# Block transposes on VectorE and sixteen SBUF transfers for two of six query tiles of a bucketed attention with a mixture of experts behind it

## The chip, the cores and the metric

One core of one Trainium2 chip runs the whole program in one launch. The metric is device microseconds (us) from start to end of an execution. The kernel before takes 754.33 us (median of three runs, 753.67 to 754.85).

## The reference

Attention over 4 batches and 8 heads, 768 tokens, 64 features a head: each query and key gets a bucket of six sign bits, and a query sees only the keys of its bucket. Behind it a mixture of eight experts, one expert for a token.

```python
def _attn_ref(q, k, v, proj):                     # q, k, v: 4 x 8 x 768 x 64, proj: 64 x 6
    q_bits = (np.einsum('bhsd,dk->bhsk', q, proj) > 0)
    k_bits = (np.einsum('bhsd,dk->bhsk', k, proj) > 0)
    q_bucket, k_bucket = (np.sum(b * 2 ** np.arange(6), axis=-1) for b in (q_bits, k_bits))
    mask = q_bucket[:, :, :, None] == k_bucket[:, :, None, :]
    scores = np.where(mask, np.matmul(q, k.transpose(0, 1, 3, 2)) / 8, -1e9)
    attn = np.exp(scores - np.max(scores, axis=-1, keepdims=True))
    attn = attn / (np.sum(attn, axis=-1, keepdims=True) + 1e-09)
    return np.matmul(attn, v)
# x: the 3072 tokens x 512 features of the above
# expert = argmax(x @ w_gate), gate = its softmax; out = gate * (relu(x @ w1[expert]) @ w2[expert])
```

## The kernel before, in words

**Groups and units.** The attention runs over 16 groups g of two heads. A group has 12 units i: a unit is 128 queries of one head against all 768 keys. Units 0 to 5 are the first half of the queries (three query tiles t of two heads s), units 6 to 11 the second half. In groups 1 to 15 units 2c and 2c+1 are the two heads of one query tile, so pair c = 0 to 5 is a query tile.

**The steps of a unit**, each a letter in a hand-written order (`HEAD` for group 0, `PLAN` for groups 1 to 14, `LAST` for group 15). The order is each engine's program order: all engines take their instructions in it, and only semaphores hold them back. A trailing `-` means the step belongs to the group before.

- S (`score`): four TensorE matmuls of 384 columns into a PSUM tile `s` (three of them). The mask comes in as 16 extra rows of the operands (line 285).
- R (`peak`, lines 295 to 297): VectorE takes the row maximum from PSUM and makes bias and scale of it. Each second R also puts work on GpSimd (`behind`): two of the twelve pieces (`split`) that prepare the operands of the next group's scores, and behind the eighth of them the two mask loads (`mask`, line 258).
- X (`expo`, line 305): ScalarE takes the exponential, `s` to the SBUF tile `e` (four of them).
- T (`trans`, line 319): for a pair c and k = 0, 1, 2, four TensorE transposes of 128 x 128 of `e` into a PSUM tile `t` (two of them, shared with all other small products).
- E (`trans_ev`, lines 343 and 345): the eviction of that tile to `pt`, by ScalarE (a) or VectorE (v).
- V (`pv`, line 355): the product of `pt` with the values, one for each half of a group, V0 and V1: 24 matmul instructions into a `t`. O (line 360) evicts it, K (`tok`, line 374) turns it into rows by token with the router's columns, L (line 384) scales and stores it with the reciprocals of M.
- G, H: the product with the six projections for the next group, and its signs on ScalarE. H also calls `lsh_bits` (line 253): GpSimd scales the bits, a transfer writes them to DRAM (`md`, line 254, SyncE's queue), and `mask` reads them back in another layout.

**Loads.** `before`, called at every second S, puts the loads of later groups on SyncE's queue: `load_x` (line 76, two of 768 KB a group), `load_pair` (line 81, 768 KB), `load_v` (line 86, 384 KB), and in groups 1 and 2 four `fill` each (line 149, 1156 KB to DRAM).

**Behind the attention.** After each batch of four groups, `route` counts the tokens of each expert and `scatter` (line 448, GpSimd's queue) writes them to DRAM sorted by expert. The experts' part (lines 641 to 799) starts at about 440 us. There, `xt_blocks` already turns 32 x 32 blocks on VectorE (line 679), from tiles that four transfers of 32 partitions each have filled (line 641).

Of the kernel before, what the change touches and what calls it, by code (L numbers as in the profile page):

```python
# [53 lines left out]
def lsh_attention_moe(ctx, tc, qk, qk2, v, proj, wg, w1, w1p, w2, out):  # L54
# [256 lines left out]
    def trans(c, k):  # L311

        i = 2 * c
        e = PP[i], PP[i + 1]
        p = ps.tile([128, 512], F32, name="t", bufs=2)
        for x in range(4):
            w, j = (x % 2, x // 2) if i in (0, 4) else (x // 2, x % 2)
            kt = 2 * k + j
            nc.tensor.transpose(p[:, x * 128:(x + 1) * 128],  # L319
                                e[w][:, kt // 3, (kt % 3) * 128:(kt % 3) * 128 + 128], ident)  # L320
        TB[c, k] = p
        if k == 2:
            del PP[i], PP[i + 1]

    def trans_ev(c, k, vec):

        p = TB.pop((c, k))
        u = c // 3
        if u not in PT:
            PT[u] = wk.tile([128, 2, NT, HALF], F32, name="pt")  # L330
        pt = PT[u]
        _, _, s, t = unit(2 * c)
        ks, q = slice(2 * k, 2 * k + 2), slice(t * 128, t * 128 + 128)
        if c in (0, 2):
            parts = [(pt[:, s, ks, t * 128:t * 128 + 256], p.rearrange("p (k q) -> p k q", k=2))]
        elif c == 1:
            parts = [(pt[:, w, ks, (2 - 2 * w) * 128:(3 - 2 * w) * 128],
                      p[:, w * 256:(w + 1) * 256].rearrange("p (k q) -> p k q", k=2)) for w in range(2)]
# [514 lines left out]
    def weight_half(op, x):  # L853
# [31 lines left out]
    """.split()  # L885

    PLAN = """
        S0 E40a- L0- X11- T41- R0 T42- E41a- S1 E42a- G X0 R1 T50- H S2 E50a- S3 X1 R2 T51- T52- E51a- S4 E52v- X2
        T00 R3 T01 E00a S5 E01a R4 T02 X3 V1- R5 X4 E02a X5 T10 O1- S6 E10a T11 R6 T12 E11a S7 E12a T20 X6 T21 E20v
        S8 E21a R7 T22 S9 E22a R8 K1- X7 V0 R9 X8 X9 M1- L1- M0 T30 O0 S10 E30a T31 R10 T32 E31a S11 E32a T40 X10  # L890
        R11 K0
    """.split()

    LAST = """
# [5 lines left out]
        r1 m6 r1 u5 u6 tV c0 m7 u7 tV d5 d6 tP c1 d7  # L900
    """.split()

    DEAL = {"R5": 1, "E12a": 2, "T20": 1, "R8": 1, "M0": 1}

    def route_step(g, w):

        b, q = divmod(g - NP, NP)
        if b < 0 or b >= B - 1:
            return
        if q == 0 and w == "M0":  # L910
            routes[b] = route(b, (0, 1))
            go(routes[b], 1)
        if q == 1:
            go(routes[b], DEAL.get(w, 0))
        if q == 2 and w in ("R0", "R2"):
            scatter(b, w == "R2")

    def before(c):

        g, r = divmod(c, 6)  # L920
        if g + 2 < NG and r in (0, 2) and g + 2 != NG - 1:
            load_x(2 * g + 4 + r // 2)
        if g == NG - 2 and r == 0:
            load_x(2 * g + 2)
            load_x(2 * g + 3)
# [4 lines left out]
        if g in (1, 2) and r > 1:  # L930
            fill((g - 1) * 4 + r - 2)

    def behind(i):

# [14 lines left out]
            weights((1, 1, 1, 2, 1, 2)[c - NC + 6])  # L949

    TK = {}

    def step(g, w):

        prev = w.endswith("-")
        w = w.rstrip("-")
        n = g - prev
        if n < 0 or (g == NG and not prev):
            return
        op, x = w[0], w[1:]  # L960
        if op == "S":
            i = 12 * n + int(x)
# [3 lines left out]
        elif op == "R":  # L966
            i = 12 * n + int(x)
            peak(i)
            behind(i)
        elif op == "X":  # L970
            expo(12 * n + int(x))
        elif op == "T":
            trans(6 * n + int(x[0]), int(x[1]))
        elif op == "E":
            trans_ev(6 * n + int(x[0]), int(x[1]), x[2] == "v")
        elif op == "V":
            for kt in range(NT):
                pv(2 * n + int(x[0]), kt)
        elif op == "O":
            pv_end(2 * n + int(x))  # L980
        elif op == "M":
            sums(2 * n + int(x))
        elif op == "K":
            TK[2 * n + int(x)] = tok(2 * n + int(x))
        elif op == "L":
            tok_ev(2 * n + int(x), TK.pop(2 * n + int(x)))
        elif op == "G" and n + 1 < NG:
            lsh_mm(n + 1)
        elif op == "H" and n + 1 < NG:
            lsh_ev(n + 1)  # L990
            if n:
                lsh_bits(n + 1)
        elif op in "kjqlp":
            cut(op, int(x[0]), int(x[1]), x[2])
        elif op == "y":
            lsh_first(int(x[0]), int(x[1]))
        elif op == "b":
            bits_first(int(x[0]), int(x[1]))
        elif op == "f":
            if x == "0":  # L1000
                before(0)
            score(0, (x == "1",))
        elif op == "i":
            if int(x[0]) not in SC:
                SC[int(x[0])] = ps.tile([128, 2, 512], F32, name="s", bufs=3)
            warmth(SC[int(x[0])][:, 0], int(x[1]))
        elif op == "s":
            split(2 + int(x[0]), int(x[1]))
        elif op == "z":
            mask(2 + int(x))  # L1010
        elif op == "w":
            lsh_bits(1)
        elif op in "xgh":
# [12 lines left out]
    last = [route(B - 1, (0,)), route(B - 1, (1,))]
    for g in range(NG):
        for w in HEAD if g == 0 else LAST if g == NG - 1 else PLAN:
            step(g, w)
            route_step(g, w)  # L1030
            if g == NG - 2 and w in ("R5", "R7", "M0", "R11"):
                next(pick, None)
                if w == "R11":
                    raw_load(0, 0)
                    raw_load(0, 1)
            if g == NG - 1 and w == "R9":
# [126 lines left out]
```

## Time and profile before

| | us |
|---|---|
| median of three runs | 754.33 |
| lowest, highest | 753.67, 754.85 |
| the profiled execution | 755.68 |
| span of its instructions | 753.9 |
| attention, groups 1 to 14: from one V0 to the next | 27.1 to 27.4 |

The profiled execution took 1.8 us more than its span from the first to the last instruction. It is 1.35 us above the median. Times of rows count from the start of the span.

### The profile page before, as it was taken

Reading aid. Unit: us, or ns where it says so; the run is one execution under the profiler, and the core shown is the slowest. Engines: PE = TensorE matmul, PEld = TensorE weight load, DVE = VectorE, ACT = ScalarE, POOL = GpSimd, SP = SyncE. Lnnn points to the kernel's source line nnn. Section 1 sums busy time; section 2 is a strip of 40 time slices with the busy share of each in tenths; the row PEclk is TensorE's granted clock in tenths of the full one; section 3 lists DMA queues with packets and bytes.
Section 4 is the critical chain, followed back from the end, with each engine's and each line's share of the span. In section 5 each row is a group of like instructions: output and inputs, shape, how many; then the busy total and the mean of one; then the engine's idle time right before and its main releaser. Section 6 shows DMA issues by size and latency. Waiting matters only on the chain.

```text
span 753.9 us, 13381 instructions
## 1 busy us (share of the span) xinstructions
PE 745.7 (99%) x4723; PEld 616.2 (82%) x4723; DVE 456.5 (61%) x1042; ACT 483.2 (64%) x942; POOL 470.5 (62%) x575
## 2 busy tenths in 40 slices
PE   9999999999999999999999999999999999999997
PEld 5778777777787787877778788889999999989896
DVE  7766766767676676676688775254383925262421
ACT  7879878878887887887887761464344444453410
POOL 6867355578635768735766643576666666668532
PEclk9999999999999999999999999999999999999999
DMA  8499844235325335422343323956636476736401
GB/s 283 168 315 277 280 128 168 83 133 193 128 64 168 121 111 200 154 75 67 101 173 116 116 73 134 253 160 189 155 135 170 144 131 181 188 135 170 147 9 38
DMA packets 60181, 113.71 MB, mean 151 GB/s; under 512 B 12227, under 2 KB 27715, under 8 KB 60112
## 3 DMA queue, kind: packets, MB, share of 16 engines
q1 hardware_dynamic: 53280, 96.47, 42.3%
q0 software_dynamic: 6688, 16.35, 6.4%
q8 instruction: 38, 0.62, 0.4%
q14 instruction: 31, 0.25, 0.1%
q10 hardware_dynamic: 144, 0.02, 0.0%
HBM read 86.98 MB, written 26.33 MB: 150 GB/s over the span
## 4 chain that ended last, share of the span: by engine, by line
PE 90%; issue 3%; DMA 2%; POOL 1%; DVE 1%; ACT 1%; POOLq 0%; DVEq 0%; SPq 0%; ACTq 0%
PE t L319 17%; PE t L355 17%; PE s L729 15%; PE s L766 10%; PE s L287 9%; PE s L285 9%; PE s L786 6%; PE t L374 3%; DMA raw<-in_w1p_dram 2%; PE t L243 2%; PE s L795 1%; POOL w L625 1%; PE t L105 1%; DVE xh L682 1%; ACT e L305 0%
## 5 line engine op out<-in xcount | busy, mean ns | idle before, releaser
L295 DVE TENSOR_REDUCE m<-s 128x1 f32<-128x768 f32 x192 | 182.9, 952 | 94.8 <-PE s L287 85.6
L305 ACT ACTIVATE e<-s,m 128x768 f32<-128x768 f32 x192 | 191.2, 996 | 16.6 <-DVE m L297 9.8
L625 POOL TENSOR_TENSOR w<-raw,w 128x512 fp32r<-128x512 f32 x112 | 144.6, 1317 | 39.7 <-ACT w L624 39.1
L345 ACT ACTIVATE pt<-t 128x512 f32<-128x512 f32 (+1 forms) x253 | 142.9, 593 | 28.9 <-PE t L319 25.1
L319 PE MATMUL t<-ident,e 128*128 128x128 f32 x1152 | 160.6, 275 | 0.6 <-ACT e L305 0.4
L319 PEld LDWEIGHTS t<-ident,e 128*128 128x128 f32 x1152 | 132.6, 140 | 33.9 <-issue 12.6
L355 PE MATMUL t<-pt,vt 128*64 128x384 f32 x768 | 130.9, 490 | 0.0
L729 PE MATMUL s<-xh,w 128*128 128x456 f32 (+6 forms) x672 | 127.0, 346 | 0.7 <-DVE xh L682 0.7
L729 PEld LDWEIGHTS s<-xh,w 128*128 128x128 f32 x672 | 119.1, 188 | 4.1 <-DVE xh L682 1.0
L355 PEld LDWEIGHTS t<-pt,vt 128*64 128x64 f32 x768 | 52.2, 137 | 62.2 <-issue 60.1
L745 DVE SCALAR_TENSOR_TENSOR hh<-s,hh 128x256 fp32r<-128x256 f32 (+7 forms) x64 | 35.5, 555 | 110.8 <-ACT hh L743 109.6
L743 ACT ACTIVATE hh<-s 128x256 fp32r<-128x256 f32 (+7 forms) x64 | 31.3, 490 | 83.1 <-PE s L729 83.1
L766 PE MATMUL s<-hh,w 128*128 128x456 f32 (+3 forms) x384 | 74.9, 355 | 0.0
L624 ACT ACTIVATE w<-raw 128x512 fp32r<-128x512 f32 x112 | 66.4, 623 | 11.7 <-DMA raw<-in_w1p_dram 11.5
L766 PEld LDWEIGHTS s<-hh,w 128*128 128x128 f32 x384 | 71.1, 188 | 2.6
L799 POOL DMA_INDIRECT out_dram<-y,ix x26 | 25.9, 998 | 62.4 <-DVE y L797 37.3
L786 PE MATMUL s<-w,hh 128*128 128x512 f32 (+1 forms) x240 | 56.7, 395 | 0.8 <-ACT hh L743 0.8
L285 PE MATMUL s<-w 80*128 80x384 f32 x192 | 57.0, 378 | 0.0
L285 PE MATMUL s<-qk 80*128 80x384 f32 x192 | 56.3, 375 | 0.0
L786 PEld LDWEIGHTS s<-w,hh 128*128 128x128 f32 (+1 forms) x240 | 44.5, 187 | 11.7 <-ACT hh L743 1.3
L287 PE MATMUL s<-qk 128*128 128x384 f32 x192 | 50.0, 341 | 0.0
L253 POOL TENSOR_SCALAR bits<-bits,wsg 64x384 f32<-64x384 f32 x15 | 18.7, 1245 | 50.2 <-ACT bits L226 50.2
(202 smaller groups left out, 1018.4 us busy)
## 6 DMA issues: line engine op xcount, KB each, us to landing
raw<-in_w_dram SPq DMA_DIRECT2D x36, 512.0 KB, 3.7
raw<-in_w1p_dram SPq DMA_DIRECT2D x28, 512.0 KB, 3.8
xd<-in_qk_dram SPq DMA_DIRECT2D x16, 768.0 KB, 4.3
xhe<-in_qk_dram SPq DMA_DIRECT2D x15, 768.0 KB, 7.6
w<-in_qk_dram SPq DMA_DIRECT2D x14, 768.0 KB, 4.4
sorted_rows<-xr SPq DMA_DIRECT2D x8, 1156.0 KB, 14.5
vt<-in_v_dram SPq DMA_DIRECT2D x16, 384.0 KB, 3.9
masks<-bits SPq DMA_DIRECT2D x15, 192.0 KB, 1.9
```

The source lines that it names most:

```text
L285: nc.tensor.matmul(p[:, a, :HALF], k[0:80, 2, c], k[0:80, 3, n], start=i >= 4, stop=i < 4)
L287: nc.tensor.matmul(p[:, a, :HALF], k[:, 0, c], k[:, 1, n], start=i < 4, stop=i >= 4)
L295: nc.vector.tensor_reduce(m[:, 0:1], p[:, :, :HALF], axis=AX.XY, op=OP.max)
L305: nc.scalar.activation(e, p[:, :, :HALF], AF.Exp, bias=m[:, 2:3], scale=m[:, 1:2], accum_out=SM[g, hf][:, t, s:s + 1])
L319: nc.tensor.transpose(p[:, x * 128:(x + 1) * 128], e[w][:, kt // 3, (kt % 3) * 128:(kt % 3) * 128 + 128], ident)
L345: nc.scalar.activation(o, x, AF.Copy)
L355: nc.tensor.matmul(p[s * 64:(s + 1) * 64, :HALF], VT[g][:, kt, s, :], PT[u][:, s, kt, :], start=(kt == 0), stop=(kt == NT - 1))
L624: nc.scalar.activation(w[:, 0, a], r, AF.Copy)
L625: nc.gpsimd.tensor_tensor(w[:, 1, a], r, w[:, 0, a], op=OP.subtract)
L729: nc.tensor.matmul(p[:, :c], w[:, a, d, fs], x[:, b, d, :c], start=(k == 0), stop=(k == 11))
L766: nc.tensor.matmul(p[:, :c], w[:, a, f % 4, ms], h[b][:, f, :c], start=(k == 0), stop=(k == 23))
L786: nc.tensor.matmul(p[:pw], HH[n][b][:, f, i:i + pw], w[:, a, f % 4], start=(k == 0), stop=(k == 23))
```

## The change

In groups 1 to 14, the pairs c = 0 and 1 (units 0 to 3) are no longer transposed by TensorE. A new step D (`blocks`) turns each of the four units in 32 x 32 blocks on VectorE, from `e` to a tile `z` (in the place of `w2`, or `w0` in group 14). After the fourth, sixteen transfers on SyncE's queue carry blocks from each quarter of 32 partitions to each other quarter of `pt`: 32 partitions of 3072 B, 98 KB each. The layout of `pt` changes so that a transfer is contiguous in it: the 384 queries of a half lie as 4 quarters of 3 tiles of 32. So the matmul of V reads its moving operand in runs of 32, the transposes write `t` in runs of 32, and the evictions write runs of 64. In group 0, whose units 0 to 5 lie in another order, each eviction of its first three pairs is two instructions of 256 columns.

The loads of a group stand together behind the transfers (step I), with two fills each in groups 1 to 4. The write of the bits to `md` goes to GpSimd's queue. `PLAN` is new: the last transposes of a group, R11, X10, X11, V0 and V1 now run in the next group, K1 and L1 in the one after it (`--`); `END` closes group 14; `DONE` keeps a step from running twice. The routing steps of a batch move to one group.

```diff
-        nc.sync.dma_start(md[g], r)
+        (nc.gpsimd if g > 1 else nc.sync).dma_start(md[g], r)
...
+        o = p.rearrange("p (a w j i) -> p j w a i", j=2, w=2, a=4)
         for x in range(4):
...
-            nc.tensor.transpose(p[:, x * 128:(x + 1) * 128],
+            nc.tensor.transpose(o[:, j, w],
                                 e[w][:, kt // 3, (kt % 3) * 128:(kt % 3) * 128 + 128], ident)
...
+    def pt_tile(u):
+        if u not in PT:
+            PT[u] = wk.tile([128, 4, 3, 2, NT, 32], F32, name="pt")
+        return PT[u]
...
+    def blocks(i):
+
+        g, r = divmod(i, 12)
+        c, w = divmod(r, 2)
+        if r == 0:
+            ZT[g] = moe.tile([128, 4, 2, 2, NT * 32], F32, name="w2" if g < NG - 2 else "w0")
+        z = ZT[g]
+        e = PP.pop(i).rearrange("p h c -> p (h c)").rearrange("p (k g j) -> p g k j", g=4, j=32)
+        nc.vector.transpose(z[:, :, c, w].rearrange("p g (k i) -> p g k i", i=32), e)
+        if r == 3:
+            pt = pt_tile(2 * g)
+            for a in range(4):
+                for q in range(4):
+                    nc.sync.dma_start(pt[32 * q:32 * q + 32, a, 0:2].rearrange("p t s k i -> p (t s k i)"),
+                                      z[32 * a:32 * a + 32, q].rearrange("p c w x -> p (c w x)"))
...
+        x = p.rearrange("p (a w x) -> p a w x", w=2, a=4)
+        if c < 3:
+            parts = []
+            for w in range(2):
+                _, _, s, t = unit(2 * c + w)
+                parts.append((pt[:, :, t, s, ks].rearrange("p a k i -> p a (k i)"), x[:, :, w]))
         else:
-            parts = [(pt[:, :, ks, q], p.rearrange("p (s k q) -> p s k q", s=2, k=2))]
+            parts = [(pt[:, :, c % 3, :, ks].rearrange("p a s k i -> p a s (k i)"), x)]
...
-            nc.tensor.matmul(p[s * 64:(s + 1) * 64, :HALF], VT[g][:, kt, s, :], PT[u][:, s, kt, :],
+            nc.tensor.matmul(p[s * 64:(s + 1) * 64, :HALF], VT[g][:, kt, s, :],
+                             PT[u][:, :, :, s, kt].rearrange("p a t i -> p t a i"),
...
     PLAN = """
-        S0 E40a- L0- X11- T41- R0 T42- E41a- S1 E42a- G X0 R1 T50- H S2 E50a- S3 X1 R2 T51- T52- E51a- S4 E52v- X2
-        T00 R3 T01 E00a S5 E01a R4 T02 X3 V1- R5 X4 E02a X5 T10 O1- S6 E10a T11 R6 T12 E11a S7 E12a T20 X6 T21 E20v
-        S8 E21a R7 T22 S9 E22a R8 K1- X7 V0 R9 X8 X9 M1- L1- M0 T30 O0 S10 E30a T31 R10 T32 E31a S11 E32a T40 X10
-        R11 K0
+        S0 R11- E32a- K1-- X10- T40- L1-- X11- S1 E40v- T41- R0 T42- E41a- S2 M1- V0- X0 R1 E42a- R2 X1 D0
+        T50- O0- D1 S3 E50a- T51- R3 T52- E51a- S4 X2 G R4 X3 S5 E52a- S6 R5 X4 V1- H D2 X5 D3 I R6 S7 O1-
+        X6 T20 R7 T21 E20a S8 E21a M0- T22 X7 R8 S9 K0- E22a R9 X8 T30 S10 E30a L0- S11 X9 R10 T31 T32 E31a
     """.split()
...
-    DEAL = {"R5": 1, "E12a": 2, "T20": 1, "R8": 1, "M0": 1}
+    DEAL = {"R4": 1, "R5": 1, "R6": 1, "R7": 1, "R8": 1, "R9": 1}
...
+    def loads(g):
+
+        if g + 2 < NG - 1:
+            load_x(2 * g + 4)
+            load_x(2 * g + 5)
+        if g + 2 < NG:
+            load_pair(g + 2)
+        if g + 1 < NG:
+            load_v(g + 1)
...
+    END = ["K1-", "L1-", "R11", "E32a", "X10", "T40", "V0", "O0", "M0", "K0"]
...
+        elif op == "I":
+            loads(n)
+            if n < 5:
+                fill(2 * n - 2)
+                fill(2 * n - 1)
```

## Rows read from the trace of the kernel before

**Rows 1.** The page: busy time by engine, TensorE's clock in 40 slices.

```profile
PE 745.7 (99%) x4723; PEld 616.2 (82%) x4723; DVE 456.5 (61%) x1042; ACT 483.2 (64%) x942; POOL 470.5 (62%) x575
...
PEclk9999999999999999999999999999999999999999
```

**Rows 2.** The chain that ended last: shares of the span by line.

```profile
PE t L319 17%; PE t L355 17%; PE s L729 15%; PE s L766 10%; PE s L287 9%; PE s L285 9%; PE s L786 6%; PE t L374 3%; DMA raw<-in_w1p_dram 2%; PE t L243 2%; PE s L795 1%; POOL w L625 1%; PE t L105 1%; DVE xh L682 1%; ACT e L305 0%
```

**Rows 3.** V0 to V0: us, PE PEld DVE ACT POOL busy, PEclk, DMA share, GB/s.

```profile
50.17:77.25 27.08, 27.08 (x190) 20.75 (x192) 18.34 (x45) 22.41 (x44) 15.31 (x19) 1.00 0.96 309
...
284.23:311.32 27.09, 27.09 (x191) 20.76 (x192) 18.33 (x45) 22.39 (x44) 19.45 (x24) 1.00 0.45 149
...
365.57:392.94 27.37, 27.37 (x197) 20.89 (x199) 19.50 (x52) 22.54 (x45) 18.65 (x32) 1.00 0.42 140
```

**Rows 4.** TensorE in order of time, within one group: start, us, instructions.

```profile
289.39 1.04 PE L319 MATMUL t<-ident,e 128*128 128x128 f32 x8
290.18 0.60 PE L285 MATMUL s<-qk 80*128 80x384 f32 x2
...
290.97 1.04 PE L319 MATMUL t<-ident,e 128*128 128x128 f32 x8
...
294.51 4.09 PE L355 MATMUL t<-pt,vt 128*64 128x384 f32 x24
298.53 0.66 PE L319 MATMUL t<-ident,e 128*128 128x128 f32 x4
```

**Rows 5.** VectorE in order of time, same group: two R one behind the other.

```profile
293.51 0.95 DVE L295 TENSOR_REDUCE m<-s 128x1 f32<-128x768 f32 x1
...
294.81 0.95 DVE L295 TENSOR_REDUCE m<-s 128x1 f32<-128x768 f32 x1
```

**Rows 6.** ScalarE in order of time, same group.

```profile
305.01 1.00 ACT L305 ACTIVATE e<-s,m 128x768 f32<-128x768 f32 x1
...
305.98 0.59 ACT L226 ACTIVATE bits<-t,small 128x384 f32<-128x384 f32 x1
306.44 0.62 ACT L345 ACTIVATE pt<-t 128x512 f32<-128x512 f32 x1
306.92 1.03 ACT L305 ACTIVATE e<-s,m 128x768 f32<-128x768 f32 x1
```

**Rows 7.** VectorE's block transposes of the experts' part, by shape.

```profile
L679 DVE STREAM_TRANSPOSE xt<-xb 128x384 f32<-128x384 f32 x12 | 6.2, 551 | 0.0
...
L679 DVE STREAM_TRANSPOSE xt<-xb 128x480 f32<-128x480 f32 x4 | 2.5, 650 | 0.0
```

**Rows 8.** Instructions by line and shape, 284.2 to 311.3 us.

```profile
L345 ACT ACTIVATE pt<-t 128x512 f32<-128x512 f32 x16 | 9.1, 596 | 1.9 <-PE t L319 1.7
...
L343 DVE COPY pt<-t 128x512 f32<-128x512 f32 x2 | 1.4, 692 | 0.7 <-PE t L319 0.6
L253 POOL TENSOR_SCALAR bits<-bits,wsg 64x384 f32<-64x384 f32 x1 | 1.2, 1244 | 5.1 <-ACT bits L226 5.1
```

**Rows 9.** GpSimd's scatter issues, 240 to 400 us.

```profile
L448 POOL DMA_INDIRECT sorted_rows<-xr,slot x12 | 12.1, 1008 | 7.6 <-DVE xr L438 5.4 <-issue 1.7 <-POOL spacer L447 0.5
```

**Rows 10.** Windows in which transfers of 32 partitions run (last columns as above).

```profile
508.00:512.00 4.00, 4.00 (x20) 3.59 (x20) 1.27 (x2) 1.76 (x4) 4.00 (x4) 1.00 1.25 177
...
511.00:512.00 1.00, 1.00 (x6) 0.90 (x5) 0.34 (x1) 0.19 (x1) 1.00 (x2) 1.00 1.22 157
```

**Rows 11.** A window in which one load of 128 partitions runs.

```profile
288.00:289.00 1.00, 1.00 (x8) 0.82 (x7) 0.00 (x0) 0.61 (x2) 1.00 (x2) 1.00 1.01 413
```

**Rows 12.** Line 641's issues on SyncE's queue: ns min/median/max.

```profile
L641 SPq DMA_DIRECT2D xb<-sorted_rows  x28: 316/333/1724, 471.4 to 691.4; - x28
```

**Rows 13.** Both mask loads (line 258) between 284 and 312 us.

```profile
DMA to landing us min/median/max: 3.1/3.6/4.0
```

**Rows 14.** Both mask loads (line 258) between 48 and 75 us.

```profile
DMA to landing us min/median/max: 7.2/7.7/8.1
```

**Rows 15.** Semaphore instructions of V on TensorE's queue: ns.

```profile
L355 PEldq EVENT_SEMAPHORE  x16: 51/51/51, 23.8 to 429.1; - x16
```

More of the change, by code (lines that the diff above doesn't have):

```diff
@@ L323, in trans @@
             del PP[i], PP[i + 1]
+    def pt_tile(u):
+        if u not in PT:
+            PT[u] = wk.tile([128, 4, 3, 2, NT, 32], F32, name="pt")
+        return PT[u]
+    ZT = {}
+    def blocks(i):
[12 more added lines that the diff above has]
+                                      z[32 * a:32 * a + 32, q].rearrange("p c w x -> p (c w x)"))
+            del ZT[g]
     def trans_ev(c, k, vec):
@@ L328, in trans_ev @@
         u = c // 3
[L329 to L338, printed above, removed]
+        pt = pt_tile(u)
+        ks = slice(2 * k, 2 * k + 2)
+        x = p.rearrange("p (a w x) -> p a w x", w=2, a=4)
[4 more added lines that the diff above has]
+                parts.append((pt[:, :, t, s, ks].rearrange("p a k i -> p a (k i)"), x[:, :, w]))
         else:
-            parts = [(pt[:, :, ks, q], p.rearrange("p (s k q) -> p s k q", s=2, k=2))]
+            parts = [(pt[:, :, c % 3, :, ks].rearrange("p a s k i -> p a s (k i)"), x)]
         for o, x in parts:
@@ L909, in route_step @@
             return
-        if q == 0 and w == "M0":
+        if q == 1 and w == "R0":
             routes[b] = route(b, (0, 1))
             go(routes[b], 1)
-        if q == 1:
-            go(routes[b], DEAL.get(w, 0))
+        elif q == 1:
+            go(routes.get(b, iter(())), DEAL.get(w, 0))
         if q == 2 and w in ("R0", "R2"):
             scatter(b, w == "R2")
+    def loads(g):
[6 more added lines that the diff above has]
+            load_v(g + 1)
     def before(c):
         g, r = divmod(c, 6)
+        if 0 < g < NG - 1:
+            if g == NG - 2 and r == 0:
+                load_x(2 * g + 2)
+                load_x(2 * g + 3)
+            return
         if g + 2 < NG and r in (0, 2) and g + 2 != NG - 1:
             load_x(2 * g + 4 + r // 2)
-        if g == NG - 2 and r == 0:
-            load_x(2 * g + 2)
-            load_x(2 * g + 3)
         if g + 1 < NG and r == 4:
@@ L929, in before @@
             load_pair(g + 2)
-        if g in (1, 2) and r > 1:
-            fill((g - 1) * 4 + r - 2)
     def behind(i):
@@ L951, in lsh_attention_moe @@
     TK = {}
+    FIRST = []
+    END = ["K1-", "L1-", "R11", "E32a", "X10", "T40", "V0", "O0", "M0", "K0"]
+    DONE = set()
     def step(g, w):
-        prev = w.endswith("-")
+        n = g - w.count("-")
         w = w.rstrip("-")
-        n = g - prev
-        if n < 0 or (g == NG and not prev):
-            return
+        if w[0] in "SRXTEVOMKLDGH":
+            z = n, w.rstrip("av")
+            if n < 0 or z in DONE:
+                return
+            DONE.add(z)
         op, x = w[0], w[1:]
@@ L973, in step @@
             trans(6 * n + int(x[0]), int(x[1]))
+        elif op == "I":
[3 more added lines that the diff above has]
+                fill(2 * n - 1)
+        elif op == "D":
+            blocks(12 * n + int(x))
         elif op == "E":
@@ L1027, in lsh_attention_moe @@
     for g in range(NG):
-        for w in HEAD if g == 0 else LAST if g == NG - 1 else PLAN:
+        for w in HEAD if g == 0 else LAST if g == NG - 1 else FIRST * (g == 1) + PLAN + END * (g == NG - 2):
             step(g, w)
             route_step(g, w)
-            if g == NG - 2 and w in ("R5", "R7", "M0", "R11"):
+            if g == NG - 2 and w in ("R5", "R7", "R8", "R10"):
                 next(pick, None)
-                if w == "R11":
+                if w == "R10":
                     raw_load(0, 0)
```

2 lines of the change are left out of this document (1 added, 1 removed).

## The prediction

> **What bounds the kernel now.** I read the page's table of engines first. TensorE is busy for 99% of the span at its full clock (2.4 GHz, granted in every slice), the other three engines for 61 to 64% [rows 1]. The chain that ended last says the same in another way: nine tenths of it are TensorE lines, and the two largest, 17% each, are the transposes of line 319 and the products of line 355, both of the attention [rows 2]. Then the attention group by group, from one V0 to the next: 27.08 to 27.37 us, TensorE busy in all of it. VectorE is busy for 18.3 us of a quiet group (19.5 where a routing runs), ScalarE for 22.4, GpSimd for 15 to 19 [rows 3]. So a group is as long as TensorE's list of work, and what leaves that list shortens the group until another chain becomes longer. DMA moves 149 GB/s in a late group, but 309 at a share of 0.96 where four fills run [rows 3]: there it is nearly full already.
>
> **What leaves TensorE.** Eight transposes take 0.79 us from their start to that of the next instruction, 99 ns each [rows 4] (the 275 ns that a group of such rows shows as the mean of one overlap). Pairs 0 and 1 have 2 x 3 x 4 = 24 of them in a group: 2.37 us. Fourteen groups: 33.2 us. The quiet group would be 27.09 - 2.37 = 24.72 us.
>
> **What other engines get.** *ScalarE* loses 5 of its 16 evictions of 596 ns [rows 3, 8]: 22.4 - 3.0 = 19.4 us. *VectorE* gets four block transposes of 768 columns. Lines of 384 and 480 columns take 551 and 650 ns, 1.03 ns a column [rows 7], so 650 + 288 x 1.03 = 0.95 us each; one copy of 692 ns goes [rows 8]: 18.3 - 0.7 + 3.8 = 21.4 us. Both fit into 24.7, VectorE with little room.
>
> **Does the new order hold TensorE back?** I walked it through one group by hand. Start to start, S takes 0.79, four transposes 0.40, V 4.02 [rows 4]; R 1.30 [rows 5]; X 0.97, an eviction 0.48 [rows 6]; an eviction frees its tile 0.6 after its start [rows 8]. With V0 at 0, TensorE reaches S3 at 4.4, G at 6.8, V1 at 9.3, S7 at 13.3, T30 at 17.6, T32 at 20.0, S0 at 20.4, S2 at 24.0. VectorE ends D1 at 4.7 and waits for S3; it ends D3 at 12.0 and R6 at 13.4, again ahead of S7. TensorE waits only a tenth each for X3 (before S6) and E22 (before T30) and nearly two for X10 (before S1): 0.3 us a group, 4.2 in all, period 25.0.
>
> **The sixteen transfers.** They start when D3 is done, at 12.0, and V0 needs them at 25.0. Behind D3 SyncE stands, and behind it the group's loads, which no one needs before the next group's R1. Sixteen issues take 0.33 us each [rows 12], 5.3 us, less than the data: 1.57 MB. The nearest rows for the rate are the loads of 32 partitions in the experts' part, 177 GB/s in four windows of 1 us, 157 in the worst, while a load of 128 partitions reaches 413 [rows 10, 11]: 8.9 us, between 3.8 and 10.0. I take 177, since each of the sixteen touches 32 partitions. With the bits and masks between them (0.39 MB, 1.2 us) and some 2 us to land, they are there at 12.0 + 0.3 + 8.9 + 1.2 + 2 = 24.4: 0.6 us in time.
>
> The rows at 177 GB/s are of short rows out of DRAM, so the partitions need not be their limit. The Trainium skill (SBUF — State Buffer, Door 1: The DMA port swizzle) says they are: 32 partitions reach half of the ports, measured there at 189 GB/s for 1 MiB, and issuing several such transfers does not join their ports. By it the sixteen take an estimated 8.3 us; by the fast row, 3.8. It speaks against splitting the move by quarters, but with 24.4 against 25.0 the sum stays the same by either.
>
> New waits on TensorE's own queue: V0 now waits for sixteen transfers. A semaphore instruction takes 51 ns [rows 15]; none to fifteen more is 0 to 0.77 us a group. I take 0.1, as most can pass while S2 still streams: 1.4 us.
>
> **Bits and masks.** H used to be early in the group; now it ends at 10.4, and S0 of the next group, which needs the first mask, stands at 20.4. In these 9.9 us GpSimd must scale the bits (1.24 [rows 8]), write them through its own queue and, when they have landed, load the masks; behind the wait stand the last four pieces of the next operands, which S0 and S1 need too. Of a write through this queue there is no row; the mask loads take 3.1 to 4.0 us to land in a quiet stretch, 7.2 to 8.1 with the DMA full [rows 13, 14]. So the chain takes from 1.3 + 3.1 + 3.1 = 7.5 to 1.3 + 8.1 + 8.1 = 17.5 us. The transfers from quarter to quarter run all through it, but they fill the engines for 9 us only: I take 4.6 and 4.2, 10.1 us, 0.2 late; 2.8 us in all.
>
> **Other terms.** *Groups with fills* (2 to 5): the sixteen at 8.9 us and the rest (2.75 MB of loads, 0.39 of bits and masks, two fills of 1.18) at the 322 GB/s that 309 at 0.96 stand for [rows 3], 17.1 us, make 26.0, 1 us over the period: 4 us in all, from 0 to 10. *Groups with scatter* (three): six issues of 1.0 us on GpSimd [rows 9] ahead of the bits, and I take 1 of the 6 us as late in each: 3 us. *Routing*: the 1.2 us by which VectorE's busy groups exceed the quiet ones [rows 3] stood in two groups of four and now stand in one, some 2 us where 3.6 are free: 0.7 each, 2 us. *Group 14* takes its V0 early, behind the transfers: 1 us. *Group 0*: six evictions become two instructions of 256 columns each, between nothing and another 596 ns [rows 8] apiece, 0 to 3.6 us; I take 0.5, since ScalarE has slack. The move of the loads costs nothing: the next group's R1 is 10 us behind.
>
> **Sum**, against the profiled execution's 755.7 (span 753.9 and 1.8 around it): 755.7 - 33.2 + 4.2 + 1.4 + 2.8 + 4 + 3 + 2 + 1 + 0.5 = 741.4. The median of the runs lies 1.35 lower: **740 us**.
>
> **Rivals.**
> *Nothing is late but the 0.3 us of the walk.* The waits hide in each other, and the transfers run nearer 413 GB/s. 755.7 - 33.2 + 4.2 - 1.35 = 725 us. For it: every chain above misses by less than a us. Against it: they all end within one us of need.
> *The masks are late, and the kernel is slower.* The place is S0, behind the second landing. Two landings of 6 us, between the quiet and the full rows, make 13.3 against 9.9: 3.4 us. A group has 1.0 us to lose (14.3 / 14), so it decides from 1.2 us of lateness on. At 1.8 (two landings of 5.2) the time is 740 + 14 x 1.6 = 762; at 3.4, 785. For it: the sixteen transfers are in flight in exactly this window. Against it: at 48 us several MB stood queued, here 1.57.
> *The sixteen transfers are late.* V0 stands still. At 110 GB/s they land at 29.8 - 2.8 = 27.0 us, 2.0 late: 740 + 14 x 2 - 2.8 (the masks hide behind it) = 765. Against it: no row of 32 partitions is below 157. For it: SyncE's issues took up to 1.7 us when its queue was full [rows 12], and a tile whose dependencies are tracked too widely would make E20 wait for them as well.
> *VectorE becomes the bound.* If a block transpose takes 1.9 us, its list is 25.2 and its waits come on top, 26.3 a group: 758.
> *Writes to PSUM in short runs are slower.* The transposes that stay now write runs of 32. If they took twice as long, 48 x 0.099 x 14 = 66 us more: 806. No matmul before writes in pieces, so no row decides. That is a rule of the Trainium skill (same page and section: PSUM has lines of 8 bytes, and any non-contiguous pattern slows matmuls); a run of 32 fills such lines, so it is unlikely.
>
> **How the numbers follow.** Forecast 0.48 (own range 728 to 752), nothing late 0.15, masks late 0.17, transfers late 0.12, VectorE 0.05, PSUM 0.03. Range: 722 to 768; below it lies a third of "nothing late", above it half of "masks late", some of "transfers late" and PSUM. 0.2%, or 1.5 us, is what a measurement of this kernel can tell. Faster: the first two and a tenth of the late ones, 0.67. Same, where a wait takes the gain: 0.06. Slower: 0.27.
>
> **What would show it.** Right: line 319 with 816 transposes and TensorE at 25 us from V0 to V0; block transposes of about 0.95 us, 56 of them; idle time of TensorE of half a us a group, put down to masks or `pt`. Wrong: TensorE idle for over a us a group ahead of line 285 (masks) or ahead of line 355 behind the transfers; VectorE busy for 24 us of a group; matmuls of line 355 above 486 ns or transposes above 99 ns apart.

## The result, and the profile after

The changed kernel takes 745.8 us (median of four runs, 743.55 to 746.45), the kernel before 754.18 beside it (753.67 to 754.85): ratio 0.9881, 95% interval 0.9865 to 0.9897, so 8.4 us or 1.1% faster. The profiled execution took 746.45 us, 744.4 of them span. Forecast were 740.0 us, 14.3 faster; the time is inside the range. All times and ratios are of executions in the faster of two states; two of the twelve of experiment 6 (1187 and 4041 us) are left out for that.

The page of the changed kernel, its engines and the shares of its chain by line:

```profile
PE 719.3 (97%) x4387; PEld 582.3 (78%) x4387; DVE 490.9 (66%) x1086; ACT 441.7 (59%) x876; POOL 478.1 (64%) x589
...
PE s L753 15%; PE t L378 15%; PE t L320 10%; PE s L790 10%; PE s L285 8%; PE s L287 8%; PE s L810 4%; DMA xhe<-in_qk_dram 3%; PE t L398 3%; PE t L243 2%; DMA raw<-in_w1p_dram 2%; ACT pt L368 1%; ACT e L305 1%; SPq L346 1%; POOL w L649 1%
```

336 instructions have left TensorE (4723 in [rows 1]) and its busy time fell by 26.4 us. But it is no longer busy all the time: 25.1 us of idleness stand where 8.2 stood. The transposes (line 320 now) went from 17% of the chain [rows 2] to 10%, and a transfer is in it that was not there: `xhe`, the load of the pair that G multiplies, 3%.

The groups by shape, whole span (busy us, mean ns, idle before):

```profile
L378 PE MATMUL t<-pt,vt 128*64 128x384 f32 x768 | 132.6, 495 | 4.9 <-DVE r L389 2.5 <-issue 2.0 <-DMA pt<-w 0.3
L320 PE MATMUL t<-ident,e 128*128 128x128 f32 x816 | 115.6, 275 | 8.4 <-ACT pt L368 7.3 <-ACT e L305 0.6 <-DVE xr L408 0.2
...
L341 DVE STREAM_TRANSPOSE w<-e 128x768 f32<-128x768 f32 x56 | 51.3, 954 | 2.2 <-DMA xd<-in_qk_dram 0.7 <-DMA w<-in_qk_dram 0.7 <-issue 0.6
```

816 transposes and 56 block transposes of 954 ns: the change does what it says, at the price worked out for it (0.95).

Windows from one V1 to the next (columns as in [rows 3]): group 1's stretch, a group with fills, one with a routing, two quiet ones, the end of group 14, and the two parts of that end around its V0.

```profile
34.50:60.00 25.50, 21.92 (x140) 15.92 (x139) 19.87 (x46) 18.93 (x38) 13.59 (x18) 1.00 0.43 104
...
95.07:121.11 26.04, 24.79 (x166) 18.58 (x168) 20.98 (x48) 19.48 (x39) 15.93 (x20) 1.00 0.91 276
147.11:173.78 26.67, 25.75 (x173) 18.28 (x175) 22.32 (x54) 19.12 (x37) 22.91 (x35) 1.00 0.94 286
199.29:224.00 24.71, 24.71 (x166) 18.16 (x168) 20.98 (x48) 19.30 (x39) 15.96 (x20) 1.00 0.65 193
...
300.52:325.23 24.71, 24.71 (x167) 18.16 (x168) 21.06 (x48) 19.08 (x39) 15.94 (x20) 1.00 0.69 192
...
376.84:410.09 33.25, 27.64 (x172) 20.53 (x174) 22.59 (x53) 19.16 (x39) 24.12 (x30) 0.95 0.56 157
...
388.00:394.71 6.71, 3.93 (x29) 3.45 (x27) 4.60 (x13) 4.07 (x9) 5.35 (x7) 1.00 0.91 191
394.71:400.50 5.79, 5.78 (x24) 2.57 (x24) 0.00 (x0) 0.00 (x0) 0.04 (x1) 0.71 0.84 300
```

These two quiet groups take 24.71 us with TensorE busy in all of it: that is 27.09 [rows 3] less the 2.37 us of 24 transposes, with nothing given back. So the gain is whole where nothing else is late. It is given back at the start (3.6 us of idle TensorE in the first window), in the groups with fills and routings, a little in the other quiet ones (of six, four take 25.0 to 25.5 us, 2.0 more in all, with waits of up to 0.7 for V0 or for `xhe`), and above all in 376.84 to 410.09, where one period takes 33.25 us.

By the start of each V1 in order of time, the same four stretches in three kernels (the forecast by the terms of the prediction, 326.03 - 12 x 2.37 + 12 x 0.6 + 9 for the second; the last column is an experiment below):

| stretch | before | forecast | after | D early |
|---|---|---|---|---|
| start to V1 of group 1 | 66.84 | 65.6 | 69.29 | 70.50 |
| V1 of group 1 to V1 of group 13 | 326.03 | 313.8 | 307.48 | 302.60 |
| V1 of group 13 to V1 of group 14 | 26.47 | 25.7 | 33.25 | 27.13 |
| V1 of group 14 to V1 of group 15 | 25.37 | 25.4 | 25.37 | 25.38 |

The middle came out 6.3 us better than forecast, the start 3.7 and the end 7.6 worse. The forecast was near because errors of both signs met in it: that is luck. One execution does not fix these stretches closely: where the code of a stretch is the same, the start took up to 70.56 and the middle up to 311.46 in the executions of experiments 3 to 5.

SyncE's queue in a quiet group, in order of time:

```profile
201.74 10.05 SPq L346 DMA_DIRECT2D pt<-w  x16
212.24 0.84 SPq L76 DMA_DIRECT2D w<-in_qk_dram  x2
213.17 0.38 SPq L81 DMA_DIRECT2D xhe<-in_qk_dram  x1
213.64 0.72 SPq L86 DMA_DIRECT2D vt<-in_v_dram  x1
```

The sixteen issues occupy SyncE for 10.05 us, 0.63 each. The pair's load is issued at 213.17; these loads land 8.0 us after issue (median), this one at 221.14, and G, one group on, comes at 221.5. V0 starts at 214.6, and the last of the sixteen, issued at 211.2, lands at 213.45. Two chains thus end 0.3 and 1.1 us ahead of their need, in a group where the trace shows no wait at all.

TensorE's longest waits (us in total, times, longest), and pieces of the chain of the span in order of time (start, us, what):

```profile
PE t L320 <- ACT pt L368: 7.3, 8, 2.3
PE t L378 <- DVE r L389: 2.5, 1, 2.5
PE t L378 <- issue: 2.0, 4, 0.7
PE t L243 <- DMA xhe<-in_qk_dram: 1.8, 3, 0.8
```

```profile
48.21 1.08 ACT e L305 x2
49.28 0.50 ACT pt L368
49.78 0.04 issue
49.82 0.67 PE t L320 x4
...
110.22 8.30 DMA xhe<-in_qk_dram
135.35 9.14 DMA xhe<-in_qk_dram
289.35 8.58 DMA xhe<-in_qk_dram
...
393.99 0.71 issue
394.71 5.80 PE t L378 x24
```

Three times the pair's load is on the chain. At the start it is ScalarE: two exponentials of X stand ahead of the eviction that frees a transpose's tile. The wait of 2.5 us that the view puts down to line 389 is V0 of group 14: line 389 had ended at 394.0, 0.7 us before V0 began. What came last then is most likely the last of the sixteen transfers: issued at 392.1, some 2.6 us to land. The four waits of V0 that the view calls "issue" (2.0 us in all) stand in groups 3, 6, 8 and 12, and most likely have the same cause.

VectorE in order of time at the end of group 14:

```profile
377.41 1.96 DVE L489 TENSOR_TENSOR key<-pb,base 128x8 f32<-128x8 f32 x1
379.40 0.74 DVE L491 COPY key_c<-key 128x8 f32<-128x8 f32 x1
380.17 0.67 DVE L492 SCALAR_TENSOR_TENSOR key<-key,desc 128x8 f32<-128x8 f32 x1
380.77 1.82 DVE L341 STREAM_TRANSPOSE w<-e 128x768 f32<-128x768 f32 x2
```

Three instructions of the last routing stand ahead of D2 and D3. They put them 3.4 us back, and with them the sixteen transfers, which begin at 382.66 and are issued until 392.73. They also put back R6, which follows D3: ScalarE waits for it, and the wait of 2.3 us in the view above is a transpose at 385.59 that waits for the eviction behind that exponential.

### The profile page after: what moved, and what is told of

Same layout as the page of the kernel before. It is cut to its first block, busy times and chain, and to the rows that moved or that the text cites. A ratio compares the mean times of both kernels' runs of the same rounds, so it can differ in the third digit from the quotient of the medians.

```text
span 744.4 us, 13012 instructions
## 1 busy us (share of the span) xinstructions
PE 719.3 (97%) x4387; PEld 582.3 (78%) x4387; DVE 490.9 (66%) x1086; ACT 441.7 (59%) x876; POOL 478.1 (64%) x589
## 4 chain that ended last, share of the span: by engine, by line
PE 78%; DMA 6%; issue 5%; ACT 3%; DVE 3%; POOL 2%; SPq 2%; POOLq 0%; DVEq 0%; ACTq 0%
PE s L753 15%; PE t L378 15%; PE t L320 10%; PE s L790 10%; PE s L285 8%; PE s L287 8%; PE s L810 4%; DMA xhe<-in_qk_dram 3%; PE t L398 3%; PE t L243 2%; DMA raw<-in_w1p_dram 2%; ACT pt L368 1%; ACT e L305 1%; SPq L346 1%; POOL w L649 1%
## 5 line engine op out<-in xcount | busy, mean ns | idle before, releaser
L378 PE MATMUL t<-pt,vt 128*64 128x384 f32 x768 | 132.6, 495 | 4.9 <-DVE r L389 2.5
L320 PE MATMUL t<-ident,e 128*128 128x128 f32 x816 | 115.6, 275 | 8.4 <-ACT pt L368 7.3
L368 ACT ACTIVATE pt<-t 128x512 f32<-128x512 f32 (+1 forms) x187 | 104.9, 582 | 23.0 <-PE t L320 20.6
L320 PEld LDWEIGHTS t<-ident,e 128*128 128x128 f32 x816 | 94.7, 140 | 25.6 <-ACT pt L368 10.8
L378 PEld LDWEIGHTS t<-pt,vt 128*64 128x64 f32 x768 | 54.8, 138 | 69.2 <-issue 57.6
L384 ACT ACTIVATE ot<-t 128x384 f32<-128x384 f32 x32 | 15.7, 490 | 63.7 <-PE t L378 63.7
L341 DVE STREAM_TRANSPOSE w<-e 128x768 f32<-128x768 f32 x56 | 51.3, 954 | 2.2 <-DMA xd<-in_qk_dram 0.7
## 6 DMA issues: line engine op xcount, KB each, us to landing
xd<-in_qk_dram SPq DMA_DIRECT2D x16, 768.0 KB, 4.7
xhe<-in_qk_dram SPq DMA_DIRECT2D x15, 768.0 KB, 8.0
w<-in_qk_dram SPq DMA_DIRECT2D x14, 768.0 KB, 5.8
```

The costliest lines, as they stand in the source:

```text
L320: nc.tensor.transpose(o[:, j, w], e[w][:, kt // 3, (kt % 3) * 128:(kt % 3) * 128 + 128], ident)
```

## The experiments

Each is the changed kernel with the edit shown, and its ratio is to the kernel before on the same chip (754.0 to 754.8 us). The changed kernel's own is 0.9881 [0.9865, 0.9897].

**1. The pair's load ahead of the x loads.** Is `xhe` the wait, or only the first of several?

```
 def loads(g):
+    if g + 2 < NG:
+        load_pair(g + 2)
     if g + 2 < NG - 1:
         load_x(2 * g + 4)
         load_x(2 * g + 5)
-    if g + 2 < NG:
-        load_pair(g + 2)
```

> The pair load stands ahead of the two loads of x behind the sixteen transfers; nothing else differs from the changed kernel (745.8 us). Theory A, the pair load lands just when line 243 needs it: its waits (1.8 us in three groups, with the waits that follow from them some 2 us) go, 743 to 744.5 us, and the load lands some 5 us ahead of line 243. Rival, DMA is full in the groups with fills and any order only moves the wait to the transfers or the loads of x: 745 to 746.5 us.

Measured: 745.37 us, ratio 0.9864 [0.9846, 0.9881]. TensorE's waits, and its chain:

```profile
PE s L285 <- DMA w<-masks: 4.2, 3, 1.9
```

```profile
121.49 4.83 DMA masks<-bits
126.61 3.75 DMA w<-masks
```

No wait for `xhe` is left, but now three first score blocks wait for the masks. The wait has moved to the next chain that ends at the same moment, and the time stays in the rival's range.

**2. D2 and D3 earlier in the walk** ("D early"): ahead of R5, V1 and H.

```
- S6 R5 X4 V1- H D2 X5 D3 I R6 S7 O1-
+ S6 D2 X4 D3 I R5 V1- H X5 R6 S7 O1-
```

> D2 and D3, and the transfers and loads behind them, stand ahead of R5 instead of behind X5: some 1.7 us earlier. Theory A, V0 and line 243 both wait for what starts at D3 with no slack: the waits ahead of V0 (0.5 to 0.7 us in three groups) and ahead of line 243 go, 742 to 744 us. Rival, VectorE is the tight one: R5 comes 1.9 us later, X5 and S8 with it, and the group gets longer, 746 to 752 us.

Measured: 734.94 us (732.37 to 736.12), ratio 0.9729 [0.9711, 0.9747]: 11 us faster than the changed kernel, 19.4 than the one before, and the fastest of all that ran. Theory A, at about three times its gain or more. A quiet group, one with fills, and the end of group 14:

```profile
196.59:221.27 24.68, 24.68 (x166) 18.12 (x168) 20.87 (x48) 19.41 (x39) 15.95 (x20) 1.00 0.68 193
110.63:136.16 25.53, 24.98 (x166) 18.09 (x168) 20.96 (x47) 19.43 (x39) 15.95 (x20) 1.00 0.94 292
373.17:400.30 27.13, 25.87 (x172) 19.53 (x174) 19.44 (x52) 19.23 (x39) 22.11 (x28) 1.00 0.65 183
```

The sixteen now start 0.8 us after V1 (322.60 behind 321.82), where they started 2.45 after it (201.74 behind 199.29). With these 1.65 us the waits for `xhe` and of V0 are gone: the groups with fills take 24.72, 24.69 and 25.52 us, the quiet ones 24.7. The last period falls from 33.25 to 27.13, because D3 now also stands ahead of the routing's three instructions. Of the 11 us, 6.1 are there and 4.9 in the middle (table above). The start took 1.2 longer in this execution and the part behind V1 of group 15 1.3 less; neither is the edit's, since V1 of group 0 came just as late in experiment 5 (44.9) and not in experiment 9 (43.4). The groups with a routing stay as they were, 26.4 to 26.6.

**3. V0, O0, M0 and K0 of group 0 moved out of `HEAD`.** Does the early V0 of group 0 cost the 3.6 us at the start?

```
-... T31 X8 V0 z1 s02 R10 X9 z0 E31v s14 M0 T32 O0 s04 S11
-E32a T40 X10 R11 K0 s05
+... T31 X8 z1 s02 R10 X9 z0 E31v s14 T32 s04 S11
+E32a T40 X10 R11 s05
```

> V0, O0, M0 and K0 of group 0 leave the head order and run in group 1 at their place in the plan. Theory A, group 1 loses some 4 us because its stretch of five transposes and five scores has no V0 to cover the evictions and the row maxima: 741.5 to 743.5 us, idle time of TensorE between 32 and 44 us below 1 us. Rival, the evictions left over from group 0 cause it, whatever stands among them: 745 to 747 us.

Measured: 747.33 us, ratio 0.9900 [0.9885, 0.9914]. TensorE is busy for all of 34.5 to 60 us, but just ahead of it, where it was idle for 0.7 us, it now is for 3.0, at a lower clock:

```profile
24.00:34.50 10.50, 7.51 (x34) 6.13 (x33) 7.61 (x19) 5.58 (x12) 9.51 (x13) 0.77 0.09 22
```

1.8 us of that is a score block at 29.39 that waits for its mask, which V0 had covered. So the idle time went away and came back elsewhere, and moving V0 gains nothing. What V0's place would cost without that wait is not shown. The chain rows at 48 us point to ScalarE, which is behind with the exponentials there; that was not tried by itself.

**4. V0 to L0 of group 14 moved from its own end into the last group.**

```
-END = ["K1-", "L1-", "R11", "E32a", "X10", "T40", "V0", "O0", "M0", "K0"]
+END = ["K1-", "L1-", "R11", "E32a", "X10", "T40"]
```
(and `M0- V0- O0- K0- L0-` in `LAST` where `PLAN` has them)

> V0, O0, M0, K0 and L0 of group 14 leave the end of group 14 and run in group 15 between its first scores, as in every other group. Theory A, V0 there waits 2.5 us for the sixteen transfers, runs at the lower clock for 1.8 us and delays what is behind it by some 1 us: 739.5 to 742 us, no lower clock. Rival, the last group's order has no room for it and the loss moves behind it: 744 to 746 us.

Measured: 747.7 us, ratio 0.9916 [0.9890, 0.9943]. V0 of group 14 runs in 4.09 us, at the full clock, but the period is still 31.6 us (380.26 to 411.89): 1.6 us came back, not the 8, and the total is no better: the waits for `xhe` were 5.9 us in this execution instead of 1.8. The rest of the long period lies ahead of V0, not in its place: the transpose behind the routing's instructions now waits 3.1 us.

**5. The routing's first step behind D3** in group 14 (at R6 instead of R5).

```
-w in ("R5", "R7", "R8", "R10")
+w in ("R6", "R7", "R8", "R10")
```

> One alteration: the first step of the routing's pick (three VectorE operations, 3.4 us) stands at R6 of group 14, behind D2 and D3, instead of R5, ahead of them. Theory A: the last period is long because the pick holds D3 up and with it the sixteen transfers of group 14; then they start some 3 us earlier, the 2.53 us wait of V0(14) shrinks, and V1(13) to V1(14) falls from 33.25 to 28.5 to 30 us; total 741 to 743. Theory B: the last period is long because the pick's 8 us of VectorE and the tokens' work must go somewhere in it; the wait only moves to another transpose or eviction, and the total stays within 1.5 us of 745.8.

Measured: 744.32 us, ratio 0.9859 [0.9844, 0.9873]. The last period falls to 30.17 us, by 3.1, about the 3.4 that the three instructions take: theory A, as to the place. Of the total only 1.5 us is seen, less than expected and inside what the intervals leave open. In this execution V1 of group 1 to V1 of group 13, where the code is the changed kernel's, took 310.85 us instead of 307.48 (311.5 and 310.9 in experiments 3 and 4). The waits for `xhe` are 5.2 to 6.0 us in these three instead of 1.8; why they differ from one execution to the next is not shown.

**6. The masks' values written back on SyncE's queue**, as in the kernel before.

```
-(nc.gpsimd if g > 1 else nc.sync).dma_start(md[g], r)
+nc.sync.dma_start(md[g], r)
```

> One alteration: the masks' values are written back on SyncE's queue as in the kernel before, not GpSimd's. Theory A: the mask chain has 2 us of slack before S0 and GpSimd only waits there anyway, so neither queue matters: 745.8, within 1.5. Theory B: on SyncE the write stands behind the sixteen transfers and the loads, 10 us, so the masks come some 8 us late and the first score block waits for them in every group: 13 groups of about 6 us, 820 or more.

Measured: 755.2 us, ratio 1.0009 [0.9995, 1.0024], no faster than the kernel before, some 9.7 us slower than the changed one. Neither theory. TensorE's waits, in an execution of 760.3 us:

```profile
PE t L378 <- DMA pt<-w: 8.3, 2, 7.8
PE t L243 <- DMA xhe<-in_qk_dram: 6.3, 4, 2.2
```

GpSimd and SyncE in group 14, and TensorE behind a wait of 2.0 us for `xhe` (columns as in [rows 3]):

```profile
395.85 1.25 POOL L253 TENSOR_SCALAR bits<-bits,wsg 64x384 f32<-64x384 f32 x1
...
397.12 0.33 SPq L254 DMA_DIRECT2D masks<-bits  x1
397.63 10.05 SPq L346 DMA_DIRECT2D pt<-w  x16
...
283.25:287.50 4.25, 4.25 (x18) 2.64 (x20) 1.09 (x2) 1.51 (x3) 4.22 (x6) 0.60 0.49 185
```

H stands ahead of D3, so SyncE now waits for GpSimd's product first and issues the write (0.33 us), and only then the sixteen. In the groups at 206.7 and 257.0 us they start 2.8 and 3.0 us after V1 instead of 2.45. In group 14, where GpSimd has the scatter ahead of the product, D3 ends at 391.2 and the sixteen start 6.5 us later; V0 waits 7.8 us, and the last period takes 36.6 us instead of 33.25. In the middle three waits of 1.9 to 2.2 us for `xhe` were paid twice: behind each the granted clock was 0.60 on average for some 4 us, between the levels of 1.2 and 2.4 GHz, and from V1 of group 1 to V1 of group 13 TensorE was busy for 308.1 us where the changed kernel's was for 300.0, with the same work. This execution is 5 us above the median, so these shares hold for it alone. The prediction did not price this move of one small transfer as a term of its own.

**7 and 8. Four more transfers of 98 KB**, to a tile that nobody reads, behind the sixteen: in the changed kernel (7) and in D early (8).

```
+dump = moe.tile([128, 768], F32, name="dump")
+for q in range(4):
+    nc.sync.dma_start(dump[32 * q:32 * q + 32], z[0:32, q].rearrange("p c w x -> p (c w x)"))
```

> One alteration: four more transfers of 98 KB from the turned block to a tile that nobody reads, behind the sixteen and ahead of the loads, in every turned group; the output is as before. By the rates of the trace they take 2.4 to 2.6 us more on SyncE's queue. Theory A: G's load of the pair, behind them, lands with no slack, so every group's G comes about 2.5 us later: 13 groups by 1.5 to 2.5 us, 765 to 778. Theory B: only the groups that already waited pay (fills and routing, seven of them), 755 to 763. Theory C: what the queue does is hidden, 746.

> The same four extra transfers in the version with D2 and D3 ahead of R5, V1- and H (734.9). Theory A: that order put the transfers about 2 us earlier, so most of the 2.5 us is covered and the rise is 2 to 10 us, to 737 to 745, well under the rise of the same transfers in the order of the changed kernel. Theory B: the gain of that order came from VectorE's order and not from the transfers' slack; then the rise is the same as there, 20 us or more.

Measured: 781.89 us (ratio 1.0362 [1.0349, 1.0375]), 36.1 over the changed kernel; and 750.82 (0.9960 [0.9947, 0.9973]), 15.9 over D early. TensorE's wait for the pair in the first and in the second:

```profile
PE t L243 <- DMA xhe<-in_qk_dram: 28.5, 12, 4.8
```

```profile
PE t L243 <- DMA xhe<-in_qk_dram: 10.7, 8, 3.7
```

From V1 of group 1 to V1 of group 13, in the changed kernel, in 7, in D early and in 8:

```profile
69.29:376.77 307.48, 300.04 (x1991) 220.09 (x1990) 257.79 (x595) 233.79 (x460) 212.37 (x293) 1.00 0.76 228
73.80:417.80 344.00, 314.18 (x1992) 226.80 (x1991) 257.62 (x593) 234.04 (x457) 206.20 (x283) 0.95 0.73 213
70.50:373.10 302.60, 299.69 (x1991) 218.10 (x1990) 256.44 (x595) 234.61 (x460) 214.89 (x296) 1.00 0.79 231
69.47:385.70 316.23, 302.49 (x1990) 220.16 (x1989) 257.44 (x595) 234.95 (x460) 212.44 (x292) 0.99 0.81 236
```

The first is theory A, larger than its numbers; the second lies between its theories, well under the rise of the first but over A's 2 to 10 us. The four take 2.5 us on SyncE's queue. In the changed kernel TensorE's idle time grows by 22.4 us in these 12 groups, 1.9 a group (1.6 against the executions of 3 to 5): most of what was added reached TensorE, so the chain from D3 over the sixteen to the pair's load has little slack there. Another 14.1 us is the same work at a lower clock. In D early the idle time grows by 10.8 us, 0.9 a group, which by the same 2.5 us leaves about 1.6 us of slack on average. It is uneven: the quiet groups waited 0 to 0.8 us for the pair, two of those with fills 3.7 and 2.6.

**9. Both moves together**: D early, and V0 to L0 of group 14 in the last group.

> Two alterations of the changed kernel together: D2 and D3 ahead of R5, V1- and H in the plan (734.9 alone), and V0, O0, M0, K0 and L0 of group 14 moved from the end of its own walk into the last group's. Theory A: behind the earlier blocks the last transfers of group 14 have landed before its V0 is reached, so there is nothing left to hide, and moving V0 only rearranges it: 735, within 1.5. Theory B: V0(14) still runs early, with nothing of the next group to cover the 1.5 us by which it is ahead of its place, and the move takes back 1.5 to 3 us: 732 to 733.5.

Measured: 735.97 us, ratio 0.9768 [0.9755, 0.9781]. Theory A: nothing more is to be had there (28.8 us from V1 to V1, 27.1 without the move).

**10. The transposes that are left done twice** for the last four units, in D early: 336 more, as many as the change took away.

```
 for x in range(4):
     ...
-    nc.tensor.transpose(...)
+    for _ in range(2 if c % 6 > 3 and 6 <= c < 90 else 1):
+        nc.tensor.transpose(...)
```

> The version with D2 and D3 early (734.9), with the TensorE transposes of the last four units of groups 1 to 14 done twice, each into the same place: 336 more of them, as many as the change took away, and nothing else is altered. Theory A: TensorE sets the pace and a transpose costs it its 99 ns there: +33 us, 766 to 770. Theory B: the pace is set by the blocks' transfers or by VectorE and ScalarE, and TensorE has room: under +20 us.

Measured: 768.0 us, ratio 1.0182 [1.0165, 1.0200]: 33.1 us for 336, 98.5 ns each. A quiet group of it:

```profile
208.99:236.17 27.18, 27.18 (x190) 20.82 (x189) 21.00 (x49) 19.57 (x39) 15.97 (x20) 1.00 0.61 175
```

So the first term of the sum, 33.2 us, is right to the tenth: theory A. TensorE sets the pace wherever nothing is late.

**11. The write of the masks on SyncE's queue, in D early** (the edit of 6 on that of 2).

> The version with D2 and D3 early (734.9), with the masks' values written back on SyncE's queue instead of GpSimd's, which cost 10 us in the changed kernel. Theory A: there SyncE's wait for GpSimd's product put the sixteen transfers 0.5 to 1 us later, and with no slack behind them that went straight into G and V0; with D3 early the write stands behind the sixteen transfers in program order, so it is not the transfers that come late but the masks: those come about 10 us later than before, some 6 to 8 us after S0 wants them, 13 groups: 800 or more. Theory B: SyncE reaches the write in time for the masks, or the walk covers it: under 745.

Measured: 970.0 us, ratio 1.2870 [1.2853, 1.2888]. TensorE's waits:

```profile
PE s L285 <- DMA qk<-masks: 104.2, 7, 22.1
PE s L285 <- DMA w<-masks: 101.0, 6, 22.1
```

Theory A, and larger: with D3 ahead of H the write stands behind the sixteen, and thirteen first score blocks wait for the masks, 16 us each. D early can only be had with the write on GpSimd's queue.

**12. The sixteen transfers cut in two**, in D early: 32 of 48 KB, the same bytes to the same places.

```
+for t in range(2):
-    nc.sync.dma_start(pt[32 * q:32 * q + 32, a, 0:2]..., z[32 * a:32 * a + 32, q]...)
+    nc.sync.dma_start(pt[32 * q:32 * q + 32, a, t]..., z[32 * a:32 * a + 32, q, t]...)
```

> The version with D2 and D3 early (734.9), with each of the sixteen transfers of a group cut in two by the pair's two pairs of units: 32 transfers of 48 KB, the same bytes to the same places. It asks what sets SyncE's 0.59 us for each of the sixteen, and so the length of the chain. Theory A: the bytes do (1.57 MB in 10.1 us): the 32 take 10 to 11.5 us together, 0.31 to 0.36 us each, and the total stays within 3 us of 734.9. Theory B: each transfer costs SyncE 0.5 us or more whatever its size: the 32 take 16 to 19 us, loads and V0 come 6 to 9 us later, of which 2 are covered, and the total goes to 790 or more.

Measured: 862.32 us, ratio 1.1422 [1.1406, 1.1437]. SyncE's queue in one group, the issues of that group by length (ns, min/median/max), and TensorE's wait:

```profile
211.10 26.61 SPq L347 DMA_DIRECT2D pt<-w  x32
```

```profile
L347 SPq DMA_DIRECT2D pt<-w x32: 507/589/1630, 211.1 to 237.1; - x32
```

```profile
PE t L379 <- DMA pt<-w: 94.5, 14, 8.1
```

Theory B, and beyond it: a transfer of 48 KB takes SyncE the same 0.59 us at the median as one of 98 KB, and 32 of them took 26.6 us, not 16 to 19. What costs on the queue is the transfer (or its 32 rows, which stayed the same), not the bytes. Fewer and larger transfers were not tried.

## Why the prediction was right, and where it was off

**What leaves TensorE, -33.2.** Right: 24.71 us in a quiet group, and 33.1 us for the same number put back (experiment 10).

**What the other engines get.** Right: 954 ns a block transpose; VectorE is busy for 21.0 us of a quiet group (21.4 worked out), ScalarE for 19.3 (19.4). VectorE is not the bound.

**The walk's waits, 4.2; semaphores of V0, 1.4; masks, 2.8.** All too high: of the six quiet groups two lose nothing, and what the other four lose (2.0 us) is waits for the sixteen and for `xhe`. The two landings of the masks took 3.2 and 4.0 us at the median, where 4.6 and 4.2 were taken. These terms make 7.2 us of the middle's 12 groups in the forecast; that is more than the 6.3 by which the middle came out better (2.3 to 2.9 in the executions of experiments 3 to 5).

**The sixteen transfers.** The step "Sixteen issues take 0.33 us each, 5.3 us, less than the data" failed: on SyncE they take 10.05 us together, and by experiment 12 it is their number that costs. The sum of that step still held. From the end of D3 to the last landing it put 12.4 us, and the trace has 11.8 in the group at 199 us (201.68 to 213.45), because the data's 8.9 us at 177 GB/s and 1.2 for bits and masks stood in the place of the issues' 10. The right length came from the wrong part, by luck.

The Trainium skill (SBUF — State Buffer, Door 1: The DMA port swizzle) puts 189 GB/s on a transfer of 1 MiB to 32 partitions; the sixteen, of 98 KB each, were issued in 10.05 us for 1.57 MB, 157 GB/s. Experiment 12 speaks against the ports as what sets this pace, since half the bytes in each transfer did not shorten its issue. The same section's rule of slower matmuls with non-contiguous PSUM patterns shows no effect here: in a quiet group all of the gain was left, and a transpose put back, which also writes runs of 32, costs 98.5 ns, against 99 before.

**"The move of the loads costs nothing: the next group's R1 is 10 us behind."** This step failed. It looked at who needs the x loads, and not at the pair's load that stands last but one in the same queue: G of the next group needs it 8.3 us after its issue, and it takes 8.0. Experiments 1, 7 and 8 show that chain: of 2.5 us added to it, 1.9 reach TensorE as idle time in the changed kernel and 0.9 in D early. The term put at nothing was 1.8 us of waits for `xhe` in the profiled execution, and 5.2 to 6.0 in those of experiments 3 to 5.

**Groups with fills, 4.** The three without a routing lost 1.0 to 1.3 us each, 3.6 in all, as forecast; but not for the reason given. With the sixteen 1.65 us earlier and all bytes the same, two of the three take 24.7 us (experiment 2). The rate of the DMA engines alone did not set their length; a chain with little slack met longer landings (8.3 to 9.1 us for `xhe`).

**Scatter and routing, 3 + 2.** The three groups lose 2.0, 1.5 and 1.9 us, 5.4 in all; D early leaves them so. In size right. The trace of D early has VectorE's R and the routing's small instructions on its chain in the group at 246 us, and not GpSimd's scatter ahead of the bits; in the one at 145 us its chain is TensorE and one eviction. Which of these decides was not tried by itself.

**Group 14, 1.** The step "Group 14 takes its V0 early, behind the transfers: 1 us" is the largest miss: the period took 7.6 us more than its forecast. Experiment 5 shows 3.1 of it as the routing's three instructions ahead of D2 on VectorE, which put back both the sixteen and R6. Experiment 4 shows 1.6 as the early V0 with its lower clock. Experiment 2 removes 6.1 in all. The prediction counted what the change adds to VectorE in a group, and not what this one group already had there between S6 and D2.

**Group 0, 0.5.** Off by 3.7 us to V1 of group 1: TensorE has five waits there of 0.7 to 1.1 us, 4.1 in all, for evictions that stand behind ScalarE's exponentials. So the reason given, "since ScalarE has slack", failed there. The twelve evictions of 256 columns are not it: eight of them ran on ScalarE, 2.7 us where four of 596 ns take 2.4, and the last had ended at 24.3, nine us ahead of the first of these waits. What in the new order brings the waits is not shown; experiment 3 shows that moving V0 out of the head does not win them back.

**GpSimd's queue for the masks.** The prediction took it as part of the mask chain only. By experiment 6 it keeps SyncE free for the sixteen, worth 9.7 us in the changed kernel; by experiment 11 it lets the masks go ahead of them, worth 235 in D early.

The rivals: none came as described. "Nothing is late" (725 us) is what two quiet groups do, and all six in D early; "the sixteen transfers are late" is, in a weak form, what the end of group 14 and the fill groups show. Its sum takes 2.8 us off a landing at 29.8 without a reason; without that its condition gives 4.8 us late and 740 + 14 x 4.8 - 2.8 = 804. Of the signs of being wrong one came, once: V0 of group 14 waited 2.5 us.

## What to carry to other kernels

When loads are moved behind a new chain in a queue, write down for every one of them when it is issued, how long it lands, and who needs it first; the one that breaks is seldom the one that was named. A group without waits can still have no slack: add a known delay to the chain and see how much of it reaches the end, as experiments 7 and 8 do, before the order is called good. Read it from the added idle time, as a part of the rise of the total can be a lower clock. And walk the irregular groups (the first, the last, those with extra work) by hand as well: here they cost more than all the regular ones.

## What the hardware showed that was not expected

A transfer from SBUF to SBUF of 32 rows took SyncE 0.59 us to issue at the median (0.51 at least), with 48 KB as with 98 KB; the transfers of 32 partitions out of DRAM took 0.33 [rows 12]. In series they came to 0.63 us (sixteen) and 0.83 us (32) each.

V0 of group 14 took 5.79 us instead of 4.02, at a granted clock of 0.71 on average between the two levels of 1.2 and 2.4 GHz; before it TensorE had been busy for 3.93 of 6.71 us (windows above). A wait on TensorE was paid twice there, once as idle time and once, 1.8 us, in the work behind it. Experiments 6 and 7 show the same in the middle of the attention: the granted clock was 0.97 and 0.95 there on average, and TensorE was busy for 8.0 and 14.1 us more than in the changed kernel with the same work.
